# A fused attention, gated layer and mixture of experts: first key load, zero writes, one set of weight bits and the order of attention changed

## Chip, cores and metric

The kernel runs on one core of a Trainium2 chip. The metric is the time of one execution on the device in microseconds, lower is better. Engines are called as in the profile: PE (TensorE), PEld (its weight loads), DVE (VectorE), ACT (ScalarE), POOL (GpSimd), SP (SyncE, which issues most DMAs). A name with a q behind it (SPq, ACTq) is an engine's sequencer, where DMAs are issued.

## What is computed

Three parts run one after the other. Cut to what matters:

```python
# attention: batch 2, heads 8, sequence 576, head size 64, mask by blocks of 64
scores = scale * q @ k^T, hidden where block_i < block_j
attn = exp(scores - max); attn /= sum(attn) + 1e-9
x = (attn @ v) as 1152 tokens x 512
# gated layer, 1536 wide
x = ((x @ w_a) * (x @ w_b)) @ w_out
# mixture: 8 experts, one for each token, capacity 288, 512 -> 1024 -> 512
expert = argmax(x @ w_gate); gate = its softmax weight
rows of x are placed by expert; h = max(x @ w1[e], 0); y = h @ w2[e]
out[token] = gate * y          # zero for tokens beyond the capacity
```

The weights of the gated layer arrive as 64-bit floats and are turned to 32 bits on the chip, by integer operations on the two halves.

## The kernel before

**Attention** treats 8 pairs of heads (pair n, batch n // 4). The steps are written out in the string `ORDER`, one word for each, in the order in which each engine gets its instructions: a word is a letter and indices. `L` loads one tensor of a pair (`load_pair`, L190: queries, keys or values, each with three buffers), `z` scales the queries on ScalarE (L199, not for pair 0), `s` computes scores of one of five row units into one of two PSUM slots, `m` takes the negated maximum on VectorE, `e` the exponential on ScalarE, `r` the reciprocal of the sums, `n` the division on GpSimd, `t` transposes on PE, `h` and `l` copy a transposed tile out of PSUM on ScalarE or VectorE, `p` multiplies with the values, `O` and `P` write the result split into a high and a low part (`xTh`, `xTl`). An engine does its steps in this order and waits where an input or a buffer is not ready. `L01`, the keys of pair 0, is the one load that ScalarE issues, with the constants behind it; all other loads stand in SP's queue.

Steps for the gated layer stand within `ORDER`: `a` loads a pair of column tiles of `w_a` and `w_b` (1 MB, three buffers `raw`), `b` and `c` turn its bits (one ScalarE instruction and four of VectorE, buffers `bits`, two of them), `H` and `I` split the result into high and low parts on ScalarE and GpSimd, and `E`, `A`, `B` compute the first half of the tokens for column tiles 0 to 2 ahead, in the same two PSUM slots as the scores, into `gE`. Before, `a`, `b` and `c` stand there for tiles 0 to 2.

At every third score step of the pairs from 1 on, `clear` (L138) writes zeros from the tile `zrow` in SBUF to a part of `xdisp` (the rows by expert, 2304 x 516) or of the output: nine writes.

**Gated layer, feed-forward** (loop over 12 column tiles f): for f below 3 only the second half of the tokens, two chunks, then four chunks of 288 tokens. A chunk is 24 matmuls of 128x288 (three products of high and low parts, four blocks, two weights), then a copy by ScalarE and a product by VectorE (`gate_mul`). Within the loop the bits of coming tiles are made (`wab_bits`), the splits (`wab_split`), and by the table `plan` at (f, place) the bits of `w_out` (`wout_bits`) and of its transpose (`wot_bits`), from which PE makes the folded gate weights (`gate_rows`, `gate_cols`). Each of the bit steps ends with `load_next`, which issues the next load of the list `later`; three are issued ahead. `raw` and `bits` buffers are shared with these loads.

Then the tokens are projected and their experts chosen, rows are scattered into `xdisp`, and the experts run.

Of the kernel before, what the change touches and what calls it, by code (L numbers as in the profile page):

```python
# [11 lines left out]
F32 = mybir.dt.float32  # L12
# [10 lines left out]
P = 128  # L23

W_MIN = struct.unpack("f", struct.pack("i", 896 << 20))[0]
W_MAX = struct.unpack("f", struct.pack("i", (1150 << 20) + 0xFFE00))[0]
G = 32
NC_IDENT, NC_TRI, NC_IOTA, NC_SEL, NC_TOK = 0, 128, 256, 264, 392


# [1 line left out]


ORDER = """
L10 z1 L01 L00 s01 m01 e010 s02 m02 e011 L11 e020 e021 s00 m00 e000 e001 s04 m04 e040 s03 m03 e030 L02 s12 r01
m12 L12 e031 r00 e120 s11 m11 e121 n010 n011 n001 t04 l04 n000 n021 L20 e111 e110 z2 n020 s10 m10 L22 s14 e101
t03 n031 m14 e140 l03 s13 e100 t02 n030 m13 e130 p05 l02 t01 l01 e131 L21 s21 t00 m21 n040 t06 h06 e210 r11 n101
n111 e211 p06 O00 l00 s20 m20 e201 s24 n110 r10 m24 t05 l05 e200 s23 e240 m23 t14 l14 n120 L30 z3 p00 s22 m22
n100 r21 p01 e231 n140 t15 l15 n130 e230 t10 n121 a0 e220 e221 p02 b0 l10 L31 s31 m31 p03 r20 e310 n131 e311 t11
l11 s32 L40 t13 m32 L41 n201 l13 t12 e321 l12 e320 p04 L32 n221 O01 s30 s34 n200 m30 e301 n210 m34 t16 h16 n220  # L40
n240 t23 P01 s33 p10 n211 P00 p15 p11 t26 n230 l23 m33 n231 e300 r31 n310 n300 e340 t22 l22 z4 s40 l26 s44 e330
m40 e331 m44 e400 t21 r30 n321 e401 t25 s42 p12 e440 p16 n340 l25 p13 O10 a1 m42 e420 l21 n301 s43 e421 P10 m43
p14 O11 P11 t20 h20 t24 l24 L50 e431 s41 e430 n311 t34 l34 z5 m41 e410 n320 L51 e411 r40 p20 n331 t31 t32 p21
l31 s52 n330 n440 b1 t30 l32 t33 m52 e520 e521 r41 n410 l33 s51 m51 p22 n411 p25 n431 h30 c10 p23 p26 p24 O20
P20 n430 s50 m50 n401 O21 L42 t36 h36 e510 t35 L60 e511 l35 e500 s54 m54 e540 P21 t44 l44 t40 e501 z6 s53 p30
m53 e530 n420 e531 l40 p35 p31 L61 s61 n400 r51 m61 e611 L52 t46 t45 h45 e610 l46 n421 p32 L70 r50 c11 n531 s60
m60 t43 e600 l43 n540 e601 n510 s64 m64 e640 t42 h42 t41 h41 p33 p36 p34 O31 s62 c12 s63 m62 n530 t51 P31 t55
O30 p40 l51 e621 e620 t56 h56 p41 n521 P30 p45 p42 z7 n501 n500 n520 m63 e630 c13 L71 s73 m73 n511 h55 p43 p46
e631 r60 n620 n630 O40 p44 O41 t50 l50 t52 h52 s74 r61 n601 e730 t54 t53 P41 p50 n621 n631 l54 e731 H1 I1 t60
m74 e740 l53 s70 m70 e700 n610 e701 P40 s72 m72 e721 L62 e720 p51 p55 p52 n640 l60 s71 m71 e710 e711 c00 p53 p56  # L50
r70 n730 n740 n611 p54 O51 r71 O50 n701 t61 h61 a2 n600 E1100 t62 h62 E1101 c01 E1000 c02 E1102 E1001 b2 E1103
n700 t65 E1110 E1002 E1111 n721 E1003 A10 h65 n731 E1112 E1010 t63 h63 c03 A11 E1113 c20 E1011 H0 P51 t64 P50
h64 E1012 t75 h75 B11 E1013 p60 c21 c22 B10 p65 p61 t70 p62 L72 p66 n720 p63 t66 l66 h70 t71 h71 I0 E0000 E0100
t76 p64 E0101 E0001 t72 c23 E0002 E0102 E0003 E0103 l72 h76 O61 E0010 E0110 O60 P60 E0011 E0111 E0012 E0112 n710
H2 A00 E0013 B00 n711 t74 P61 t73 l73 I2 E2100 E0113 E2101 A01 B01 p70 h74 p75 p71 p76 O70 p72 E2000 p73 E2102
E2001 E2103 E2002 p74 E2003 E2110 E2010 O71 E2111 E2011 P70 E2112 P71 E2012 A21 E2113 B21 E2013 A20 B20
"""

HIDDEN = -1e30
# [2 lines left out]
def const_columns(n_tok, n_exp):  # L62
# [9 lines left out]
    for i in range(P):  # L72
        c[i, NC_SEL + i % G] = 1.0
    c[:, NC_TOK::3] = np.arange(P)[:, None] + P * np.arange(nt)[None, :]
# [1 line left out]


@with_exitstack
def fused_kernel(ctx: ExitStack, tc, shape, q, k, v, w_a, w_b, w_out, w_gate, w1, w2, w_outT, consts, out, cap):
    nc = tc.nc  # L80
    B, H, S, D = shape
    NTOK, DM = out.shape
# [8 lines left out]
    NF = DFF // P  # L91
# [3 lines left out]
    NTT = (S + P - 1) // P  # L95
    ROW = DM + 4
    NSLOT = E * cap
    FAR = 1 << 20
    CH = S // 2
    NCH = NTOK // CH  # L100
    EARLY = 3
# [9 lines left out]

    wgp = cpool.tile([P, KD, G], F32, name="wgp")
    nc.vector.memset(wgp, 0.0)
    xdisp = dpool.tile([NSLOT, ROW], F32, name="xdisp")
# [11 lines left out]
    att1 = es_a.enter_context(tc.tile_pool(name="att1", bufs=1))  # L126
# [2 lines left out]
    psX = es_p.enter_context(tc.tile_pool(name="psX", bufs=2, space=PSUM))  # L129
    psD = es_p.enter_context(tc.tile_pool(name="psD", bufs=1, space=PSUM))  # L130
    psS = es_p.enter_context(tc.tile_pool(name="psS", bufs=1, space=PSUM))


    zrow = att1.tile([P, ROW], F32, name="zrow")
    nc.gpsimd.memset(zrow, 0.0)
    nc.gpsimd.memset(zrow[:, DM + 1:DM + 2], float(FAR))

    def clear(dst, w, r0, cnt):  # L138
        nc.sync.dma_start(
            out=dst[r0:r0 + cnt * P, :].rearrange("(c p) d -> p c d", p=P),  # L140
            in_=zrow[:, 0:w].unsqueeze(1).to_broadcast([P, cnt, w]),
        )

# [44 lines left out]
    def load_pair(n, j):  # L190
        kept, src, w = ((qT, q, NU * P + 2 * ODD), (kT, k, S), (vT, v, NTT * 2 * D))[j]
        kept[n] = att.tile([P, w], F32, tag="qkv"[j], name=f"{'qkv'[j]}T{n}", bufs=3)
        if (n, j) == (0, 1):
            nc.scalar.dma_start(out=kept[n], in_=src[n])
            nc.scalar.dma_start(out=cst, in_=consts)
        else:
            nc.sync.dma_start(out=kept[n], in_=src[n])
# [110 lines left out]
    def pv(n, r):  # L308
# [5 lines left out]
        vt = vT[n].rearrange("p (t c) -> p t c", t=NTT)  # L314
        for m in range(2 * D // G):
            nc.tensor.matmul(
                pxs[n, bank][m * G:(m + 1) * G, a - c0:c1 - c0], lhsT=vt[:, t, m * G:(m + 1) * G],
                rhs=PT[n][:, t, m * G // D, a:c1],
                start=(t == 0), stop=(t == (1, NTT - 1)[bank]), skip_group_check=True,
# [97 lines left out]
        a=load_wab, b=lambda f: bits_wab(f, 0), c=lambda f, i: bits_wab(f, i + 1), H=hi_wab, I=lo_wab,  # L417
        E=ahead, A=ahead_copy, B=ahead_mul,
    )
    clears = [(xdisp, ROW, r, min(3, (NSLOT - r) // P)) for r in range(0, NSLOT - P + 1, 3 * P)]  # L420
    clears += [(out, DM, r, min(3, (NTOK - r) // P)) for r in range(0, NTOK, 3 * P)]
    if NSLOT % P:
        clears.append((xdisp, ROW, NSLOT - P, 1))
    n_score = 0
    for word in ORDER.split():
        steps[word[0]](*map(int, word[1:]))
        if word[0] == "s" and int(word[1]) >= 1:
            if n_score % 3 == 0 and clears:
                clear(*clears.pop(0))
            n_score += 1  # L430
    assert not clears
    nc.sync.dma_start(out=wgp[:, :, 0:E], in_=w_gate.rearrange("(k p) e -> p k e", p=P))
    es_a.close()

# [5 lines left out]

    Wp = gp.tile([P, NF, G], F32, name="Wp")

# [63 lines left out]
    def gate_mul(f, c, pa, pb):  # L506
# [3 lines left out]

    es_p.close()

    later = [
        (load_wab, 3), (load_wab, 4), (load_wab, 5), (load_wot, 0), (load_wab, 6), (load_wout, 0), (load_wab, 7),
        (load_wot, 1), (load_wab, 8), (load_wout, 1), (load_wab, 9), (load_wot, 2), (load_wab, 10), (load_wout, 2),
        (load_wab, 11), (load_wot, 3), (load_wout, 3), (load_wot, 4), (load_wout, 4), (load_wot, 5), (load_wout, 5),
    ]
# [1 line left out]
    def load_next():  # L519
        if later:  # L520
            fn, i = later.pop(0)
            fn(i)

    for _ in range(3):
        load_next()
    nc.sync.dma_start(out=g_sb[:, 0:EARLY, 0:S], in_=gE)

    def wab_bits(f):
        for part in range(5):
            bits_wab(f, part)  # L530
        load_next()

    def wab_split(f):
        hi_wab(f)
        lo_wab(f)

    def wot_bits(c):
        bits_wot(c)
        load_next()

    def wout_bits(c):
# [2 lines left out]


    plan = {
        (2, 3): [(wot_bits, 0)], (3, 1): [(gate_rows, 0), (wout_bits, 0)], (3, 2): [(split_wout, 0)],
        (3, 3): [(gate_cols, 0)],
        (4, 1): [(wot_bits, 1)], (5, 0): [(gate_rows, 1)], (5, 1): [(wout_bits, 1)],
        (5, 2): [(gate_cols, 1), (split_wout, 1)],  # L550
# [8 lines left out]
    with tc.tile_pool(name="psF", bufs=3, space=PSUM) as psF, tc.tile_pool(name="psW", bufs=1, space=PSUM) as psW:  # L559
        for f in range(NF):  # L560
            order = list(range(NCH)) if f >= EARLY else [3, 2]
            for i, c in enumerate(order):
                pp = []
                for j in range(2):
                    ps = psF.tile([P, CH], F32, tag=f"p{j}", name=f"p{j}_{f}_{c}")
                    prod(ps, f, j, c, range(KD))
                    pp.append(ps)
                gate_mul(f, c, *pp)
                place = NCH - len(order) + i
                if i == 0 and f + 3 < NF:  # L570
                    wab_bits(f + 3)
                if i == len(order) - 1 and f + 3 < NF:
                    wab_split(f + 3)
                for fn, x in plan.pop((f, place), ()):
                    fn(x)
            del wab[f]
    assert not plan and not later
    es_x.close()


# [34 lines left out]
    def small(name, shape, dt=F32):  # L615
# [6 lines left out]
        out=tail4[:, :, 1:ROW - DM], in_=cst[:, NC_TOK:NC_TOK + 3 * NT].rearrange("p (t c) -> p t c", c=3)  # L622
# [33 lines left out]
    def place():  # L656
        pp = psG.tile([P, NT + 1, E], F32, tag="pp", name="pp")
        nc.tensor.matmul(pp, lhsT=tri, rhs=oh, start=True, stop=False)
        for t in range(NT):
# [19 lines left out]
        nc.vector.tensor_scalar(  # L679
            out=far, in0=pos, scalar1=float(cap), scalar2=float(FAR), op0=ALU.is_ge, op1=ALU.mult  # L680
        )
# [479 lines left out]
```

## Time and profile before

| | us |
|---|---|
| median of 3 runs | 488.49 |
| lowest, highest | 487.98, 491.27 |
| the profiled execution | 488.28 |
| its span, first to last instruction | 486.5 |
| PE busy | 440.7 |
| DVE busy | 253.5 |
| ACT busy | 191.2 |
| POOL busy | 133.5 |

The profile is of one execution. Times are counted from the first instruction. Busy times of PE hold modelled ends of matmuls, so they are read against the length of a stretch and not as a rate. The granted clock of PE is a share of 2.4 GHz. The chain of work that ended last, which the profile follows back from the last instruction, ends after less than 1 us here, so the stages are read from waits and from windows instead.

### The profile page before, as it was taken

What the parts mean: (1) busy time and instruction counts of PE and PEld (TensorE: products, weight loads), DVE (VectorE), ACT (ScalarE), POOL (GpSimd) and SP (SyncE); (2) the same over time, 40 slices, a digit from 0 to 9 for tenths busy, and PEclk for the clock granted to TensorE, in tenths of its full rate; (3) what the DMA queues carried; (4) which work ended last, traced back from release to release, by engine and by line L of the source; (5) the groups of instructions that cost most, each with busy time, mean ns of one, the idle gap of its engine ahead of it and who ended that gap; (6) DMA issues with size and microseconds to landing.
All of it is one profiled execution on the core that took longest, in us unless ns stands there. A gap on an engine that the chain in (4) does not pass through costs nothing. (4 is left out here: it accounts for less than half of the span.)

```text
span 486.5 us, 8343 instructions
## 1 busy us (share of the span) xinstructions
PE 440.7 (91%) x3248; PEld 358.0 (74%) x3248; DVE 253.5 (52%) x401; ACT 191.2 (39%) x382; POOL 133.5 (27%) x146
## 2 busy tenths in 40 slices
PE   0689999989999699999999999999994999999993
PEld 0245455577799599999999968888883988979750
DVE  0567877784257866676866716221203672826110
ACT  1466667753233344434334322131303563715100
POOL 0067676595011131312221012331212001001000
PEclk9989999999999799999999999999996899999997
DMA  8660971622043545555342000497004983563880
GB/s 275 206 222 8 352 291 33 199 88 86 1 141 110 174 170 174 173 174 172 111 151 88 1 1 0 122 389 292 24 5 128 368 291 126 169 203 111 315 329 11
DMA packets 42986, 76.43 MB, mean 157 GB/s; under 512 B 2850, under 2 KB 15266, under 8 KB 42928
## 3 DMA queue, kind: packets, MB, share of 16 engines
q1 hardware_dynamic: 41296, 71.90, 44.1%
q0 software_dynamic: 1344, 3.29, 1.8%
q8 instruction: 30, 0.49, 0.4%
q10 hardware_dynamic: 288, 0.51, 0.3%
q14 instruction: 28, 0.23, 0.1%
HBM read 64.41 MB, written 11.46 MB: 156 GB/s over the span
## 5 line engine op out<-in xcount | busy, mean ns | idle before, releaser
L395 PE MATMUL p<-xTh,hi 128*128 128x288 f32 x336 | 101.2, 301 | 1.0 <-DVE gE L411 1.0
L395 PE MATMUL p<-xTh,lo 128*128 128x288 f32 x336 | 99.9, 297 | 0.0
L395 PE MATMUL p<-xTl,hi 128*128 128x288 f32 x336 | 99.8, 297 | 0.0
L275 POOL TENSOR_TENSOR PB<-PB,rs 128x128 f32<-128x128 f32 (+4 forms) x72 | 58.4, 842 | 48.1 <-DVE rs L269 47.1
L395 PEld LDWEIGHTS p<-xTh,hi 128*128 128x128 f32 x336 | 64.0, 190 | 4.1 <-issue 2.9
L395 PEld LDWEIGHTS p<-xTl,hi 128*128 128x128 f32 x336 | 64.0, 190 | 0.0
L395 PEld LDWEIGHTS p<-xTh,lo 128*128 128x128 f32 x336 | 63.9, 190 | 0.0
L259 ACT ACTIVATE PB<-sc,nm 128x256 f32<-128x256 f32 (+4 forms) x72 | 39.1, 549 | 34.8 <-DVE nm L249 13.9
L249 DVE TENSOR_REDUCE nm<-sc 128x2 f32<-128x512 f32 (+4 forms) x40 | 32.3, 809 | 32.0 <-PE sc L234 17.3
L388 POOL TENSOR_TENSOR lo<-bits,hi 128x1024 fp32r<-128x1024 f32 x12 | 29.3, 2439 | 65.4 <-ACT hi L382 60.3
L722 PE MATMUL py<-woh,gh 128*128 128x512 f32 x108 | 42.6, 395 | 0.0
L722 PE MATMUL py<-wol,gh 128*128 128x512 f32 x108 | 42.3, 392 | 0.0
L722 PE MATMUL py<-woh,gl 128*128 128x512 f32 x108 | 42.3, 392 | 0.0
L850 PE MATMUL ph<-xt,hi 128*128 128x288 f32 x192 | 41.0, 308 | 0.4 <-ACT xt L817 0.4
L234 PE MATMUL sc<-kT,qT 64*64 64x448 f32 (+7 forms) x256 | 26.9, 471 | 14.7 <-DMA kT<-in_k 11.6
L451 DVE TENSOR_TENSOR gl<-g_sb,gh 128x1536 fp32r<-128x1536 f32 x9 | 15.8, 1756 | 38.4 <-ACT gh L450 38.4
L509 DVE TENSOR_TENSOR g_sb<-asb,p 128x288 f32<-128x288 f32 x42 | 18.8, 451 | 32.2 <-PE p L395 25.8
L835 DVE TENSOR_TENSOR lo<-rawA,hi 128x1024 fp32r<-128x1024 f32 x20 | 24.0, 1224 | 21.7 <-ACT hi L834 21.7
L850 PEld LDWEIGHTS ph<-xt,hi 128*128 128x128 f32 x192 | 33.2, 201 | 1.2 <-ACT xt L817 0.5
L508 ACT COPY asb<-p 128x288 f32<-128x288 f32 x42 | 16.8, 399 | 42.0 <-PE p L395 42.0
L361 POOL TENSOR_TENSOR wol<-wob,woh 128x1024 fp32r<-128x1024 f32 x6 | 14.4, 2399 | 64.3 <-ACT woh L360 53.8
L283 PEld LDWEIGHTS pT<-cst,PB 128*128 128x128 f32 x200 | 22.6, 142 | 12.3 <-issue 5.6
(163 smaller groups left out, 824.3 us busy)
## 6 DMA issues: line engine op xcount, KB each, us to landing
rawA<-in_moe_w SPq DMA_DIRECT2D x18, 1024.0 KB, 8.2
raw<-in_moe_w_a SPq DMA_DIRECT2D x12, 512.0 KB, 4.0
raw<-in_moe_w_b SPq DMA_DIRECT2D x12, 512.0 KB, 5.0
wtr<-in_w_outT SPq DMA_DIRECT2D x6, 1024.0 KB, 5.2
wor<-in_moe_w_out SPq DMA_DIRECT2D x6, 1024.0 KB, 5.0
xdisp<-zrow SPq DMA_DIRECT2D x6, 774.0 KB, 6.0
rawB<-in_moe_w SPq DMA_DIRECT2D x4, 1024.0 KB, 6.6
fs<-in_moe_w SPq DMA_DIRECT2D x4, 1024.0 KB, 10.8
```

What stands on the lines that cost most here:

```text
L234: nc.tensor.matmul(ps[i * BLK:(i + 1) * BLK, h, 512 - w:512 - w + seen], lhsT=qT[n][hs, u * P + i * BLK:u * P + (i + 1) * BLK], rhs=kT[n][ ...
L249: nc.vector.tensor_reduce(out=nm, in_=view, op=ALU.max, axis=ax, negate=True)
L259: nc.scalar.activation(out=dst, in_=src, func=AF.Exp, bias=nms[n][:, c:c + 1], accum_out=SM[n % 2][:, c, 0:1], scale=scale if unscaled(n) ...
L275: nc.gpsimd.tensor_tensor(out=x, in0=x, in1=rss[n, int(bt)][:, c:c + 1].to_broadcast(list(x.shape)), op=ALU.mult)
L283: nc.tensor.transpose(pt[:, j * P:(j + 1) * P], PB[n % 2][:, a:a + P], ident)
L388: nc.gpsimd.tensor_tensor(out=lo, in0=f32(m), in1=f32(hi), op=ALU.subtract)
L395: nc.tensor.matmul(ps, lhsT=wx[:, kd], rhs=xx[:, kd, cs], start=(kd == 0 and n_ == 0), stop=(kd == KD - 1 and n_ == 2),)
L508: nc.scalar.copy(asb, pa)
L509: nc.vector.tensor_tensor(out=g_sb[:, f, c * CH:(c + 1) * CH], in0=asb, in1=pb, op=ALU.mult)
L722: nc.tensor.matmul(s["py"], lhsT=lt[:, f], rhs=rt[:, f], start=(f == 0 and i == 0), stop=(f == NF - 1 and i == 2))
L835: nc.vector.tensor_tensor(out=lo[:, a:a + 2], in0=raw[:, a:a + 2], in1=f32(hi[:, a:a + 2]), op=ALU.subtract)
L850: nc.tensor.matmul(ph[:, 0:cap], lhsT=lt, rhs=rt, start=(n_ == 0), stop=(n_ == len(seq) - 1))
```

## The change

1. `load_pair(0, 0)` and `load_pair(0, 1)`, queries and keys of pair 0, are issued ahead of the first word of `ORDER`, in which they were the fourth and third word.
2. `zrow`, its two fills on GpSimd and the nine writes from it within attention go. The host passes an array `empty` (128 x 516) with the same content; the nine writes are issued from it, DRAM to DRAM, in the feed-forward: one behind each load of `load_next`, from the point where fewer than 14 loads are left.
3. The load and the bits of the fourth column tile (`a3`, `b3`, `c30` to `c33`) are made within attention. In the feed-forward the tiles of `wab_bits` come one step earlier: f + 4 at f = 0 and 1, none at f = 2, and `wot_bits` 0 moves from place (2, 3) to (2, 2).
4. `ORDER` is another permutation of the steps; four copies of transposed tiles go from VectorE to ScalarE.

```diff
-L10 z1 L01 L00 s01 m01 e010 s02 m02 e011 L11 e020 e021 s00 m00 e000 e001 s04 m04 e040 s03 m03 e030 L02 s12 r01
...
+L10 z1 s01 m01 e011 e010 s03 m03 e030 e031 s02 m02 e020 e021 s00 m00 L21 s04 m04 e000 e001 r01 n010 n001 n011
+L11 s13 m13 e040 r00 L20 z2 e130 e131 s10 n040 n020 m10 e101 n021 e100 n000 s14 m14 e140 t04 l04 n031 t06 l06
+s11 m11 e110 t05 l05 s12 e111 m12 t03 h03 r11 e121 t02 s20 m20 a0 L31 e201 s24 l02 m24 L02 e120 r10 n030 e200
+n111 t01 t00 l00 e240 n110 p05 L30 n131 s21 m21 h01 s23 m23 n100 e211 e210 a1 r21 n140 t11 h11 n120 z3 p00 e231
...
+e301 n201 b2 c20 c21 e731 c22 c23 e730 r70 H2 n721 E1100 E1001 E1101 E1002 E1102 l62 I2 E1003 E1103 E1010 A10
...
+h66 E0102 b3 n630 E2002 n730 n701 E0103 n740 A01 E2003 E0110 O51 t61 O50 l61 t65 l65 E2010 c30 n731 E0111 t60 h60
+E2011 E0112 t64 E2012 t76 E0113 P51 p60 n711 P50 l64 p65 c31 l76 p61 p66 p62 E2013 p63 p64 B01 A20 B20 L72 t74
...
-    zrow = att1.tile([P, ROW], F32, name="zrow")
-    nc.gpsimd.memset(zrow, 0.0)
-    nc.gpsimd.memset(zrow[:, DM + 1:DM + 2], float(FAR))
...
+    load_pair(0, 0)
+    load_pair(0, 1)
     for word in ORDER.split():
         steps[word[0]](*map(int, word[1:]))
-        if word[0] == "s" and int(word[1]) >= 1:
-            if n_score % 3 == 0 and clears:
-                clear(*clears.pop(0))
-            n_score += 1
...
+    def clear():
+        dst, w, r0, cnt = clears.pop(0)
+        nc.sync.dma_start(
+            out=dst[r0:r0 + cnt * P, :].rearrange("(c p) d -> p c d", p=P),
+            in_=empty[:, 0:w].unsqueeze(1).to_broadcast([P, cnt, w]),
+        )
...
     later = [
-        (load_wab, 3), (load_wab, 4), (load_wab, 5), (load_wot, 0), (load_wab, 6), (load_wout, 0), (load_wab, 7),
+        (load_wab, 4), (load_wab, 5), (load_wot, 0), (load_wab, 6), (load_wout, 0), (load_wab, 7),
...
             fn(i)
+        if len(later) < 14 and clears:
+            clear()
...
-        (2, 3): [(wot_bits, 0)], (3, 1): [(gate_rows, 0), (wout_bits, 0)], (3, 2): [(split_wout, 0)],
+        (2, 2): [(wot_bits, 0)], (3, 1): [(gate_rows, 0), (wout_bits, 0)], (3, 2): [(split_wout, 0)],
...
-                if i == 0 and f + 3 < NF:
-                    wab_bits(f + 3)
+                ahead_ = 4 if f < EARLY else 3
+                if i == 0 and f != EARLY - 1 and f + ahead_ < NF:
+                    wab_bits(f + ahead_)
                 if i == len(order) - 1 and f + 3 < NF:
                     wab_split(f + 3)
```

## Rows read from the trace of the kernel before

**Rows 1.** Windows by stage: stretch, length, busy us (instructions) by engine, clock, DMA

```profile
12.00:36.00 24.00, 18.07 (x125) 8.08 (x117) 13.94 (x30) 12.85 (x45) 7.83 (x12) 0.93 0.67 220
36.00:98.00 62.00, 58.01 (x654) 31.92 (x655) 48.16 (x90) 42.38 (x127) 41.42 (x51) 1.00 0.52 173
98.00:134.00 36.00, 32.98 (x302) 27.07 (x302) 18.36 (x27) 13.49 (x29) 16.60 (x14) 1.00 0.19 59
172.00:250.00 78.00, 78.00 (x600) 76.28 (x599) 54.35 (x69) 31.65 (x50) 21.48 (x9) 1.00 0.48 155
```

**Rows 2.** Timeline of the start, three engines: start, us, instruction, idle before and releaser

```profile
0.74 0.88 SPq L197 DMA_DIRECT2D qT<-in_q  x2
0.75 1.28 ACT L200 ACT_TABLE_LOAD   x1 [0.75 <-PEq L1122]
3.82 0.74 ACT L200 ACTIVATE qT<-qT 128x640 f32<-128x640 f32 x1 [1.79 <-DMA qT<-in_q]
3.83 0.39 ACTq L194 DMA_DIRECT2D kT<-in_k  x1
11.65 2.41 PE L234 MATMUL sc<-kT,qT 64*64 64x192 f32 x16 [11.65 <-DMA kT<-in_k]
19.57 3.66 PE L234 MATMUL sc<-kT,qT 64*64 64x448 f32 x16
```

**Rows 3.** DMA issues: what, queue, count, KB each, median us from issue to landing

```profile
kT<-in_k ACTq DMA_DIRECT2D x1, 288.0 KB, 7.7
xdisp<-zrow SPq DMA_DIRECT2D x6, 774.0 KB, 6.0
out<-zrow SPq DMA_DIRECT2D x3, 768.0 KB, 9.5
wtr<-in_w_outT SPq DMA_DIRECT2D x6, 1024.0 KB, 5.2
```

**Rows 4.** The tile of queries: the landing of its loads

```profile
DMA to landing us min/median/max: 3.0/3.8/10.1
```

**Rows 5.** Timeline of PE: the wait of the first `gate_rows`

```profile
164.42 1.08 PE L494 MATMUL pw<-wtb,wgp 128*32 128x256 f32 x8 [4.66 <-DVE wtb L355]
```

**Rows 6.** Windows behind that wait

```profile
164.40:166.40 2.00, 1.98 (x12) 1.17 (x13) 1.93 (x4) 0.83 (x2) 0.00 (x0) 0.50 0.34 94
166.40:168.40 2.00, 2.00 (x10) 2.00 (x10) 1.97 (x2) 0.60 (x1) 0.00 (x0) 0.50 1.09 379
168.40:170.40 2.00, 2.00 (x12) 2.00 (x11) 1.93 (x5) 0.40 (x1) 0.00 (x0) 0.58 0.44 82
```

**Rows 7.** Window of attention in which zeros and weights were moved

```profile
48.00:60.00 12.00, 10.82 (x119) 5.86 (x118) 9.24 (x19) 7.60 (x26) 7.45 (x11) 1.00 1.02 333
```

**Rows 8.** Timelines of SP, ACT, DVE, PE: gate part 1 from load to use

```profile
168.66 0.37 SPq L477 DMA_DIRECT2D wtr<-in_w_outT  x1
179.68 1.17 ACT L343 ACTIVATE wtb<-wtr 128x1024 f32<-128x1024 f32 x1
182.80 0.69 DVE L345 TENSOR_SCALAR wtb<-wtb 128x1024 f32<-128x1024 f32 x1
184.25 1.23 DVE L351 SCALAR_TENSOR_TENSOR wtb<-wtr,wtb 128x1024 int32<-128x1024 int32 x1
185.51 1.22 DVE L355 SCALAR_TENSOR_TENSOR wtb<-wtr,wtb 128x1024 int32<-128x1024 int32 x1
190.40 0.64 PE L494 MATMUL pw<-wtb,wgp 128*32 128x256 f32 x8
```

**Rows 9.** Timeline of DVE within attention

```profile
108.85 3.29 DVE L351 SCALAR_TENSOR_TENSOR bits<-raw,bits 128x1024 int32<-128x1024 int32 x1
```

**Rows 10.** Timeline of DVE: last instructions of two sets of bits

```profile
155.69 1.22 DVE L355 SCALAR_TENSOR_TENSOR bits<-raw,bits 128x1024 int32<-128x1024 int32 x1
163.14 1.23 DVE L355 SCALAR_TENSOR_TENSOR wtb<-wtr,wtb 128x1024 int32<-128x1024 int32 x1
```

**Rows 11.** Window of the feed-forward, first matmul to first logits

```profile
134.06:282.97 148.91, 143.64 (x1081) 139.51 (x1081) 103.66 (x126) 57.25 (x91) 36.35 (x18) 0.98 0.41 134
```

## What was predicted

> **What bounds the kernel now.** I read the busy time of the engines by stage first [rows 1]. In each row the reader compares PE's busy time with the length of the stretch. From 36 to 98 us PE is busy 58.01 of 62.00, from 98 to 134 us 32.98 of 36.00, from 172 to 250 us all of it. TensorE is the limit there, and no other engine comes near: VectorE, the next, has 48.16, 18.36 and 54.35. What can be won lies where PE stands still, and the rows of the page add up to three places.
>
> The first is the start. The queues and engines in order of time [rows 2] show that the first matmul of the kernel runs at 11.65, released by the load of `kT`. The cause stands above it: the keys of pair 0 are loaded by ScalarE's queue, and ScalarE issues that load at 3.83, after its scaling of pair 1's queries (step `z1`), which started at 3.82 when those queries landed. The load then takes 7.7 us to land, against 3.0 for the quickest load of queries [rows 3, 4], because everything that SP had issued meanwhile (values, keys, a zero write of 774 KB) shares the DMA engines with it.
>
> The second is the softmax chain of the first pair: 12 to 36 us has 18.07 of 24 busy, with two score slots in PSUM that PE fills and ScalarE empties [rows 1].
>
> The third lies in the feed-forward, which begins at 134.06. At 164.42 the first `gate_rows` has waited 4.66 us for VectorE to end the bits of `wtb` [rows 5]: PE went dry at 159.76. Behind it the granted clock reads 0.50, 0.50 and 0.58 in three windows of 2 us [rows 6], after which it is 1.00 again (2.4 GHz; 0.50 is the 1.2 GHz level).
>
> **First keys ahead of all.** Removed: ScalarE's wait for `z1` before the key load. SP now starts with pair 0's queries, ScalarE with its keys, both at 0.74 to 0.75 as the first DMA and the first ScalarE instruction do in [rows 2]. 288 KB of keys and 320 KB of queries travel together, with pair 1's queries and the constants behind. Bounds for the landing: 3.0 us (the quickest query load) and 7.7 us (this load as it was) [rows 3, 4]. The neighbours are the first query loads, so I take 3.9, which puts the first matmul at 4.65. If the table load (1.28 us) stands ahead of the issue, it is 5.9. I carry 5.0: the start moves by 11.65 - 5.0 = 6.6 us. Bounds: 0.75 + 3.0 = 3.75 (7.9 won) and 0.75 + 1.28 + 7.7 = 9.7 (1.9 won). What is late next: pair 1's first score, which stands in a run of scores at 19.57, 7.9 us after the first one [rows 2], needs `q1` and `k1`. The queue ahead of it (q0, k0, constants, q1, k2, k1, q2) is 2.1 MB, at 333 GB/s [rows 7] 6.4 us: landed by about 9, against some 13. Hidden. Pair 0's values now stand on SP behind the keys of pair 3, whose buffer is free only after pair 0's last score; that score is PE's fifth step of the new order, the first reader of the values its twentieth. I cost it at nothing; if the cover fails, it is one landing, 3.0 us or more.
>
> **Zeros taken out of attention.** The two fills of `zrow` on GpSimd go, and nobody waits for them. Nine writes leave SP's queue there. What loads gain by that can only come out of PE's idle time, which is 4.0 us from 36 to 98 [rows 1]; I take none of it here.
>
> **Fourth weights' bits within attention.** Added there: one ScalarE absolute value, 1.17 us, and four VectorE instructions, 182.80 to 186.73 = 3.9 us undisturbed [rows 8]; the third of the four, 1.23 us there, took 3.29 in attention [rows 8, 9], so 3.9 to 6. They stand at the end of the new order, in 98 to 134 us, where VectorE has 36.00 - 18.36 = 17.6 us free and ScalarE 22.5 [rows 1]. Price zero. Behind them on VectorE's queue the copies of transposed tiles and the products that free PE's score slots; if all the cover were gone, PE would wait up to the longest, 3.3 us.
>
> What it gives back in the feed-forward is a slot. Up to the wait, VectorE makes one set of bits for each of the three half columns: the third set (`bits` of weights 5) ends at 156.9 and the fourth (`wtb`) at 164.4 [rows 10]. Without the first of them `wtb` takes the third slot, since the diff moves it from place (2, 3) to (2, 2). It then ends 156.9 - 134.06 = 22.8 us into the stage. PE asks for it after eight chunks of (159.76 - 134.06) / 8 = 3.21 us, at 25.7 us. Margin 2.9 us, so the wait goes: 4.66 us. One new condition: two `bits` buffers, and the third slot needs the one that GpSimd's subtraction of weights 4 releases. That subtraction starts at the end of the column before, so the slot is not moved by more than the margin. With the wait the slow clock goes. It lasted from 164.4 to about 170.1 (2.0 + 2.0 and 84% of 2.0 us), 5.7 us at half rate, worth 2.8 us. Sum for this part 7.5 us; the stage falls from 148.9 [rows 11] to 141.4. Bounds: 0 (a wait of the same size elsewhere) and 7.5.
>
> **Zeros in the feed-forward.** Six writes of 774 KB and three of 768 KB, 7.1 MB, DRAM to DRAM, one behind each load from the seventh `load_next` on. By the plan these stand at (3, 0), (3, 1), (4, 0), (4, 1), (5, 0), (5, 1), (6, 0), (6, 1), (7, 0): 27 to 81 us into the stage. The weight loads queue behind them. The DMA engines are 0.48 busy from 172 to 250 us [rows 1]. No row shows a DRAM to DRAM copy. From below: 333 GB/s at a share of 1.02 while SBUF zeros and weights were moved [rows 7], 326 GB/s full, so 7.1 MB take 21.8 us of all engines, 0.40 of the 54 us. 0.48 + 0.40 = 0.88: it fits. From above: 9.5 us for each write, the landing of `out<-zrow` [rows 3], taken as if nothing ran beside it, 85 us or 3.9 times that. Then the load is 0.48 + 1.57 = 2.05, and the stage falls 54 x 1.05 = 57 us behind. A delay is felt late: `wtr` of gate 1 was issued at 168.66, lands in 5.2 and was first read at 179.68 (5.8 us spare), and its bits ended at 186.73 for a PE that came at 190.40 (3.7 spare) [rows 3, 8]: 9.5 us in all. I take the lower bound, since both sides of such a copy are long rows as in the loads, and cost it at nothing.
>
> A rule of the Trainium skill speaks against this part: DMA: Bandwidth & Descriptors, section Rules for kernel authors, holds that a zero-stride broadcast of a few copies as the outermost dimension confines a DMA to that many engines. The source is such a broadcast of three, though the code writes the 128 rows outermost. No run here shows which it becomes; by the rule the third rival below would hold, by the rows the sum stays.
>
> **New order.** PE's instructions are the same 200 steps, so its work stays. What an order can change is PE's idle time: 5.9 us in 12 to 36, 4.0 in 36 to 98, 3.0 in 98 to 134, 12.9 in all [rows 1], and it can as well add to it. I take 0 and keep 5 us either way.
>
> **Sum.** 488.28 (the profiled execution; its span is 486.5, and the median of the runs is 488.49) - 6.6 - 7.5 = 474.2. Against the median that is 2.9% less.
>
> **Rivals.**
> (1) The attention gives the start back: the new order's chain of score, maximum, exponential and transposes makes PE wait as much again. For it: 12 to 36 us is bound by that chain and not by PE. Against: 36 to 134 us is 93% PE. Time 488.3 - 7.5 = 480.8.
> (2) The zeros take back what the bits gave. With a copy at 2 times the price of the lower bound the load is 0.48 + 0.80 = 1.28, the stage falls 54 x 0.28 = 15 us behind, less 9.5 spare is a wait of 5.6 us, with slow clock behind it again about 7.5. Time about 481.7. Against: one engine's time goes by bytes in every row.
> (3) Slower: the zeros make the feed-forward wait for DMA. It decides from the point where the backlog is 14.1 + 9.5 = 23.6 us, that is from 1 + 23.6/54 = 1.44 of load, a price of 2.4 times. On three engines out of 16 it is 5.3 times: 0.48 + 2.1 on those, 54 x 1.6 = 86 us behind, 77 of wait, some 550 us. For it: no copy of this kind is in the trace, and the nine writes stand in one FIFO with the weights. Against: the same shape from SBUF reached 333 GB/s together with loads.
> (4) More: the order also takes 5 of the 12.9 us of idle. 469.
>
> **Chances.** Forecast 0.60, (1) 0.13, (2) 0.12, (3) 0.06, (4) 0.09. The forecast's own range is 470 to 478: 1 us of the start to the good, 3 of it and of the order to the bad. The range reaches down to (4) and up past (1) and (2): 468.5 to 482.5. About 1% (4.9 us) is what a measurement of this kernel can tell from no change, so faster means under 483.6. Forecast, (4), 0.8 of (1) and 0.6 of (2) lie there: 0.87; within 1% 0.07; slower, rival (3), 0.06.
>
> **What the profile after would show.** Start: the first L234 matmul at about 5 instead of 11.65, still released by `kT`; above 8 the landing was mis-sized. Order: the first feed-forward matmul at about 127.5; at 134 rival (1). Bits: no wait of PE for `wtb`, clock 1.00 behind it, the stage 141 to 142 us long. Zeros: landing of `xdisp<-empty` under 10 us, and loads of `wtr` read without a wait; waits of PE for `wtb` or of ScalarE for a DMA there show (2) or (3). Everything behind the feed-forward should keep its length; if it does not, the sum is wrong in a place that I did not look at.

## The result, and the profile after

The changed kernel takes 471.88 us (median; 470.74 to 472.54), the one before 488.56 beside it. The ratio is 0.9651 with a 95% interval of 0.9613 to 0.9689, so 3.5% less. The forecast was 474.2, its range 468.5 to 482.5. The profiled execution of after took 472.4 us, 15.9 less than the one that the sum was made against.

The windows by stage come first. Columns are the stretch, its length, busy us (instructions) of PE, PEld, DVE, ACT and POOL, the granted clock of PE, the DMA engines' mean share and GB/s. They answer to [rows 1] and, in the last line, to [rows 11].

```profile
12.00:36.00 24.00, 19.90 (x141) 9.96 (x145) 12.97 (x28) 13.42 (x44) 12.78 (x18) 0.73 0.38 124
36.00:98.00 62.00, 55.79 (x644) 34.59 (x637) 48.38 (x87) 46.10 (x133) 37.12 (x47) 1.00 0.37 118
98.00:126.00 28.00, 27.23 (x269) 22.98 (x268) 13.55 (x25) 8.06 (x18) 10.35 (x12) 1.00 0.21 69
126.18:267.80 141.62, 141.03 (x1080) 137.38 (x1080) 101.23 (x122) 56.99 (x90) 36.68 (x18) 1.00 0.57 184
```

The last line is the feed-forward. It is 141.62 us long instead of 148.91 and PE is busy in 141.03 of them, at full clock: the one wait of PE that is left is 0.6 us at its end. Its DMA share is 0.57 instead of 0.41, which is the zeros. The third line ends where the feed-forward begins, 7.88 us earlier than before (134.06). In the second, PE stands still 6.2 us instead of 4.0; in the third 0.8, where before it was 3.0.

The timeline of the start (start, us, queue or engine, instruction, in brackets the idle time before and what ended it), which answers to [rows 2]:

```profile
0.75 0.40 ACTq L185 DMA_DIRECT2D kT<-in_k  x1
0.75 0.90 SPq L188 DMA_DIRECT2D qT<-in_q  x2
1.18 0.45 ACTq L186 DMA_DIRECT2D cst<-consts  x1
1.66 1.28 ACT L191 ACT_TABLE_LOAD   x1 [1.66 <-PEq L1124]
5.07 2.83 PE L225 MATMUL sc<-kT,qT 64*64 64x192 f32 x16 [5.07 <-DMA qT<-in_q]
6.27 0.74 ACT L191 ACTIVATE qT<-qT 128x640 f32<-128x640 f32 x1 [3.33 <-DMA qT<-in_q]
12.03 2.29 PE L214 MATMUL sc<-kT,qT 128*128 128x288 f32 x4 [0.60 <-DVE nm L240]
```

The keys go out at 0.75, ahead of ScalarE's table load, and the first matmul runs at 5.07 instead of 11.65. In this execution the queries landed last and released it; in other kernels with the same first loads (e4, e6, e7, e9) the keys did.

The timeline of the bits of `wtb` in the feed-forward, with the subtraction on GpSimd beside them, and the matmul that reads them (its line of the waits is gone; before, PE stood still 4.66 us there [rows 5]):

```profile
140.21 2.40 POOL L379 TENSOR_TENSOR lo<-bits,hi 128x1024 fp32r<-128x1024 f32 x1 [3.81 <-ACT hi L373]
142.63 1.19 ACT L334 ACTIVATE wtb<-wtr 128x1024 f32<-128x1024 f32 x1 [1.43 <-POOL lo L379]
145.78 1.23 DVE L342 SCALAR_TENSOR_TENSOR wtb<-wtr,wtb 128x1024 int32<-128x1024 int32 x1
146.62 2.65 POOL L379 TENSOR_TENSOR lo<-bits,hi 128x1024 fp32r<-128x1024 f32 x1 [4.02 <-ACT hi L373]
147.04 3.31 DVE L346 SCALAR_TENSOR_TENSOR wtb<-wtr,wtb 128x1024 int32<-128x1024 int32 x1
151.81 0.64 PE L477 MATMUL pw<-wtb,wgp 128*32 128x256 f32 x8
```

The bits end at 147.04 + 3.31 = 150.35, 24.2 us into the stage, and PE comes for them at 151.81, 25.6 us into it. They are in time by 1.5 us.

The DMA issues of the zeros (what, queue, count, KB each, median us from issue to landing), and the stretch of 60 us in which they travel, in the columns of the windows:

```profile
xdisp<-empty SPq DMA_DIRECT2D x6, 774.0 KB, 9.2
out<-empty SPq DMA_DIRECT2D x3, 768.0 KB, 8.1
```

```profile
155.00:215.00 60.00, 60.00 (x462) 58.86 (x461) 43.56 (x55) 24.89 (x39) 16.53 (x7) 1.00 0.88 281
```

The DMA engines are busy 0.88 of that stretch, at 281 GB/s, and PE all of it.

### The profile page after: what moved, and what is told of

The parts are those of the page before. It is cut to its first block, busy times and chain, and to the rows that moved or that the text cites. A ratio compares the mean times of both kernels' runs of the same rounds, so it can differ in the third digit from the quotient of the medians.

```text
span 470.6 us, 8325 instructions
## 1 busy us (share of the span) xinstructions
PE 435.6 (93%) x3248; PEld 357.4 (76%) x3248; DVE 249.1 (53%) x397; ACT 193.3 (41%) x386; POOL 126.8 (27%) x144
## 5 line engine op out<-in xcount | busy, mean ns | idle before, releaser
L386 PE MATMUL p<-xTh,hi 128*128 128x288 f32 x336 | 100.1, 298 | 0.6 <-DVE gE L402 0.6
L266 POOL TENSOR_TENSOR PB<-PB,rs 128x128 f32<-128x128 f32 (+4 forms) x72 | 53.3, 769 | 47.9 <-DVE rs L260 44.8
L386 PEld LDWEIGHTS p<-xTh,hi 128*128 128x128 f32 x336 | 63.0, 188 | 3.3 <-issue 2.5
L225 PE MATMUL sc<-kT,qT 64*64 64x64 f32 (+7 forms) x256 | 25.5, 467 | 12.1 <-ACT PB L250 7.0
L274 PE MATMUL pT<-cst,PB 128*128 128x128 f32 x200 | 30.1, 284 | 0.9 <-ACT PT L297 0.8
```

Of the source, the lines that this page charges most:

```text
L225: nc.tensor.matmul(ps[i * BLK:(i + 1) * BLK, h, 512 - w:512 - w + seen], lhsT=qT[n][hs, u * P + i * BLK:u * P + (i + 1) * BLK], rhs=kT[n][ ...
L266: nc.gpsimd.tensor_tensor(out=x, in0=x, in1=rss[n, int(bt)][:, c:c + 1].to_broadcast(list(x.shape)), op=ALU.mult)
L274: nc.tensor.transpose(pt[:, j * P:(j + 1) * P], PB[n % 2][:, a:a + P], ident)
L386: nc.tensor.matmul(ps, lhsT=wx[:, kd], rhs=xx[:, kd, cs], start=(kd == 0 and n_ == 0), stop=(kd == KD - 1 and n_ == 2),)
```

## Experiments

All are told by three times: the median of the runs, the start of the first feed-forward matmul (T0), and the length of the feed-forward from there to the first logits (`pl`), the last two from the one profiled execution of each. The row of before gives the range of the medians of its four sets of runs. Executions of kernels that are alike up to T0 (after, e5, e8, e9, e10) have it between 125.37 and 126.27, so smaller differences than 0.9 us at T0 say little.

| | median us (range) | ratio to before, 95% | T0 | feed-forward |
|---|---|---|---|---|
| before | 488.05 to 488.95 | 1 | 134.06 | 148.9 |
| after | 471.88 (470.74 to 472.54) | 0.9613 to 0.9689 | 126.18 | 141.6 |
| e7 keys alone | 480.78 (479.50 to 481.90) | 0.9791 to 0.9866 | 128.52 | 147.8 |
| e1 keys as before | 477.50 (476.51 to 478.93) | 0.9718 to 0.9810 | 131.51 | 141.7 |
| e2 bits as before | 479.50 (478.75 to 480.61) | 0.9762 to 0.9851 | 126.16 | 148.8 |
| e3 old order | 474.49 (473.86 to 475.38) | 0.9664 to 0.9754 | 128.01 | 141.7 |
| e4 zeros in attention | 472.01 (471.43 to 472.36) | 0.9613 to 0.9699 | 125.55 | 141.7 |
| e5 zeros twice | 502.11 (501.56 to 503.07) | 1.0239 to 1.0306 | 125.81 | 170.0 |
| e8 zeros twice, apart | 473.96 (471.87 to 476.43) | 0.9647 to 0.9738 | 125.37 | 143.3 |
| e9 copies outermost | 518.47 (518.14 to 519.10) | 1.0564 to 1.0640 | 126.27 | 187.9 |
| e6 warm clock | 471.12 (468.91 to 472.54) | 0.9609 to 0.9676 | 123.04 | 141.7 |
| e10 after again | 472.23 (471.27 to 473.07) | 0.9625 to 0.9681 | 125.96 | 141.7 |
| e11 warm from start | 469.71 (468.84 to 470.25) | 0.9579 to 0.9633 | 122.71 | 141.7 |

### The keys

The kernel before with this part of the change alone (e7), and the kernel after without it (e1).

```diff
 # e7, on the kernel before
-L10 z1 L01 L00 s01 ...
+L10 z1 s01 ...
+    load_pair(0, 0)
+    load_pair(0, 1)
     for word in ORDER.split():
 # e1, on the kernel after
-L10 z1 s01 ...
+L10 z1 L01 L00 s01 ...
-    load_pair(0, 0)
-    load_pair(0, 1)
```

> The kernel before with one part of the change alone: first queries and keys ahead of the order. Sum of the prediction: 488.5 - 6.6 = 481.9. Rival (parts of the gain need the others, such as the zeros gone from the queue or the new order): 484 or more.

> The changed kernel, but the first queries and keys stand in the order again as fourth and third word (L10 z1 L01 L00). Sum of the prediction: the first matmul is back at 11 to 12 us, everything behind moves by 6.6 us, 478.5 us against 471.9 of the changed kernel. Rival (the attention would have given the start back, bound by something later): 474 or less.

The first matmul of e7, by the timeline of PE, and then of e1 the two loads that SP issues just before the keys, the issue of the keys, and the first matmul:

```profile
4.91 2.41 PE L234 MATMUL sc<-kT,qT 64*64 64x192 f32 x16 [4.91 <-DMA kT<-in_k]
```

```profile
3.09 0.43 SPq L359 DMA_DIRECT2D raw<-in_moe_w_a  x1
3.62 0.46 SPq L359 DMA_DIRECT2D raw<-in_moe_w_b  x1
3.63 0.40 ACTq L185 DMA_DIRECT2D kT<-in_k  x1
10.44 2.84 PE L225 MATMUL sc<-kT,qT 64*64 64x192 f32 x16 [10.44 <-DMA kT<-in_k]
```

Alone, the keys bring the first matmul forward by 6.7 us (11.65 to 4.91), T0 by 5.5 us (134.06 to 128.52) and the kernel by 8.1 us of medians (488.91 beside it). So 1.2 us of the start were given back within attention, a small part of rival (1). The feed-forward of e7 is 1.1 us shorter, and its rows show where. These are PE's wait for `wtb` and the two windows behind it:

```profile
158.89 1.08 PE L496 MATMUL pw<-wtb,wgp 128*32 128x256 f32 x8 [4.66 <-DVE wtb L355]
158.87:160.87 2.00, 1.98 (x12) 1.18 (x13) 1.93 (x4) 0.84 (x2) 0.00 (x0) 0.50 0.30 88
160.87:162.87 2.00, 2.00 (x13) 2.00 (x13) 1.97 (x2) 0.74 (x2) 0.00 (x0) 0.71 1.08 377
```

The wait is as long as before, but the lower clock behind it lasts 3.2 us (2.0 and 58% of 2.0) where the prediction read 5.7 in the kernel before [rows 6]; half of the difference is 1.2 us. Why it ended sooner is not shown. The rest of the 8.1 us lies behind the feed-forward (0.8 in the profiled executions) and in the spread of the runs. The expectation was 481.9, and 480.78 was measured.

In the new kernel the late keys cost 5.3 us at T0, all of the 5.4 us by which the first matmul is later; 478.5 was expected and 477.50 measured. There the keys land at 10.44 and not at 11.65, though they are issued at 3.63, about as late as before. What travels beside them differs: no zero write and no values stand in SP's queue, but 1 MB of weights, issued just before. Which of these brings them in sooner was not tested.

### The bits

```diff
 # e2, on the kernel after: a3 b3 c30 c31 c32 c33 out of ORDER, and
+        (load_wab, 3), (load_wab, 4), (load_wab, 5), (load_wot, 0), ...
-        (2, 2): [(wot_bits, 0)], ...
+        (2, 3): [(wot_bits, 0)], ...
+                if i == 0 and f + 3 < NF:
+                    wab_bits(f + 3)
```

> The changed kernel, but the fourth weights' load and bits are made in the feed-forward again, as before (plan and the load list too). Sum of the prediction: PE waits some 4.7 us for wtb again and then runs at the slow clock for some 5.7 us, 7.3 us in all: 479.2. Rival (what the bits cost in attention comes back, so that the part is worth less): 474 to 476.

The wait of PE is back, by the timeline of PE and the window of the feed-forward in e2:

```profile
156.53 1.08 PE L455 MATMUL pw<-wtb,wgp 128*32 128x256 f32 x8 [4.67 <-DVE wtb L324]
126.16:274.93 148.77, 143.48 (x1081) 139.35 (x1081) 103.91 (x126) 57.23 (x91) 36.37 (x18) 0.98 0.55 182
```

The wait is 4.67 us, as it was 4.66 before, and the eight matmuls behind it take 1.08 instead of 0.64 us. The stage is 7.1 us longer than after's, the median 7.5 above that of e4, which was timed beside it; 479.2 was expected and 479.50 measured. T0 does not move (126.16): within attention these bits cost nothing. The zeros are in this stage as well (share 0.55), so the wait and its removal have nothing to do with them.

### The order

```diff
 # e3, on the kernel after: ORDER of before, without L01 L00, and
-... c03 A11 ... E0100 t76 ... E0102 E0003 ... E0110 O60 ... E0112 n710 ... B01 p70 ...
+... c03 a3 A11 ... E0100 b3 t76 ... E0102 c30 E0003 ... E0110 c31 O60 ... E0112 c32 n710 ... B01 c33 p70 ...
```

> The changed kernel with the order of before, the first loads ahead of it and the new steps a3, b3 and c30 to c33 put in near its end. Prediction (the order is worth nothing): 471.9 to 473.2, since the start moved by 6.6 us and the feed-forward's begin by 7.9. Rival (the new order carries a part of what the start gave): 475 to 479.

T0 is 128.01, 1.8 us later than after's; the median is 2.5 above that of e4, which was timed beside it and does not overlap it. The new order is worth about 2 us, and the expected 471.9 to 473.2 was too little. The old order also takes back the engine of 36 copies of transposed tiles: in the new one 20 of them had gone from VectorE to ScalarE and 16 the other way, four more on ScalarE in all. So the order and the place of the copies are tested together. The window of the tail of attention in e3, and then all from the first matmul to T0, in e3 and in after:

```profile
98.00:128.01 30.01, 27.06 (x257) 21.37 (x257) 18.16 (x24) 10.13 (x20) 11.95 (x10) 1.00 0.33 106
5.00:128.01 123.01, 109.53 (x1080) 67.81 (x1080) 86.02 (x150) 70.35 (x201) 66.18 (x75) 0.97 0.35 117
```

```profile
5.07:126.18 121.11, 107.07 (x1080) 69.05 (x1080) 78.76 (x146) 71.87 (x205) 60.24 (x75) 0.94 0.36 118
```

In the tail PE stands still 3.0 us, as in the kernel before, against 0.8 in after. From 36 to 98 it is the other way round (58.03 busy in e3, 55.79 in after). From the first matmul to T0 the idle time is about the same in both, 13.5 and 14.0, and what is won lies in PE's busy time, 109.5 and 107.1, which holds modelled ends. How the order wins them is not settled.

### The zeros

First their place: `zrow` and its nine writes back in attention, none in the feed-forward, everything else as after (e4).

```diff
+    zrow = att1.tile([P, ROW], F32, name="zrow")
...
+        if word[0] == "s" and int(word[1]) >= 1:
+            if n_score % 3 == 0 and clears:
+                clear(*clears.pop(0))
...
-        if len(later) < 14 and clears:
-            clear()
```

> The changed kernel, but the zeros are written from SBUF within attention as before, none in the feed-forward. Prediction (zeros cost nothing in either place once the first keys are ahead of them): 471.9, within 1. Rival A (they delayed loads in attention): 474 or more. Rival B (DRAM to DRAM zeros cost in the feed-forward): 470 or less.

The same stretch of the feed-forward without zeros, in e4:

```profile
155.00:215.00 60.00, 60.00 (x462) 58.86 (x461) 42.94 (x54) 25.23 (x40) 17.14 (x8) 1.00 0.53 175
```

The median is 472.01, as expected, and the stage is 141.7 us long: the place of the zeros changes nothing that can be measured. In the feed-forward they raise the DMA share from 0.53 to 0.88 and the rate from 175 to 281 GB/s, and PE has 60.00 busy of 60.00 in both. Both places hide them.

Then their price, by making each write twice: to the same place (e5), and to other memory (e8).

```diff
 # e5
+        for _ in range(2):
             nc.sync.dma_start(out=dst[r0:r0 + cnt * P, :]...
 # e8
+    scr = [dpool.tile([3 * P, ROW], F32, name=f"scr{i}") for i in range(9)]
...
+        nc.sync.dma_start(
+            out=scr[len(clears)][0:cnt * P, 0:w].rearrange("(c p) d -> p c d", p=P),
+            in_=empty[:, 0:w].unsqueeze(1).to_broadcast([P, cnt, w]),
+        )
```

> The changed kernel, each of the nine zero writes issued twice in the feed-forward. By the prediction's own formula (0.40 of the DMA engines for each set): load 0.48 + 0.80 = 1.28, 15 us behind, less 9.5 us spare is 5.6 us of PE waiting, with the slow clock 477 to 480. Rival (a delay is absorbed further than I counted, since the loads' readers wait without PE noticing): 472 to 473. Rival (such a copy costs more than its bytes): above 485.

> The changed kernel with a second write of zeros of the same size behind each of the nine, into other memory that nobody reads, so that SP does not wait for the first to land as it did with zeros written twice to one place (502.1, SP 7 to 10 us in each pair). By the prediction's formula the DMA engines would be loaded 1.28 for 54 us, 15 us behind, less 9.5 spare: 5.6 us of PE waiting, 477 to 480. Rival (the 30 us were the price of such copies and not of SP's wait): 490 or more. Rival (absorbed): 472 to 473.

e5 missed its expectation by over 20 us. SP's own queue in e5 shows why, by three of its pairs and by the line of its waits (us in total, times, longest):

```profile
155.04 7.34 SPq L506 DMA_DIRECT2D xdisp<-empty  x2
163.63 9.72 SPq L506 DMA_DIRECT2D xdisp<-empty  x2
174.06 10.59 SPq L506 DMA_DIRECT2D xdisp<-empty  x2
SPq L506 <- DMA xdisp<-empty: 49.2, 6, 9.5
```

A pair of writes to the same rows holds SP for 7 to 11 us, where one issue takes 0.57 in after: by the line of the waits SP stands until the first has landed, 49.2 us for the six pairs of `xdisp`, and every weight load behind stands still with it. The waits that follow are ScalarE's for `wtr` and PE's for `wtb` (19.2 us in two). So e5 measured a wait in a queue and not the price of the copies. e8 has no such wait and gives the price, by its window and by the rows at its one wait of PE for `wtb` (ScalarE, GpSimd, VectorE, PE):

```profile
155.00:215.00 60.00, 60.00 (x462) 58.86 (x461) 42.84 (x54) 24.86 (x39) 16.65 (x7) 1.00 1.06 350
222.06 1.12 ACT L335 ACTIVATE wtb<-wtr 128x1024 f32<-128x1024 f32 x1 [4.93 <-DMA wtr<-in_w_outT]
225.74 2.41 POOL L380 TENSOR_TENSOR lo<-bits,hi 128x1024 fp32r<-128x1024 f32 x1 [8.27 <-ACT hi L374]
225.94 3.30 DVE L347 SCALAR_TENSOR_TENSOR wtb<-wtr,wtb 128x1024 int32<-128x1024 int32 x1
229.38 0.64 PE L478 MATMUL pw<-wtb,wgp 128*32 128x256 f32 x8 [1.57 <-DVE wtb L347]
```

Twice the bytes make the stage 1.7 us longer in the profiled execution. The runs alone do not separate e8 from after: 471.87 to 476.43 against 471.27 to 473.07 of e10, timed beside it. The median of 473.96 lies under the 477 to 480 that the formula gave and far under the 490 of the rival. The loads are late, as the formula says: ScalarE waits 4.93 us for `wtr`. But the bits now fall beside a subtraction of GpSimd, and the last VectorE instruction takes 3.30 us where it takes 1.23 alone [rows 8]. These 2.1 us are more than PE's 1.6, so by these rows (an estimate) the late load alone would still have been covered. The formula with the rate that was reached comes out near: 7.1 MB in 60 us are 118 GB/s, so the loads and two sets of copies ask for 175 + 2 x 118 = 411 GB/s, and the engines move 350; they fall 60 x 61 / 350 = 10.5 us behind, 1.0 more than the 9.5 us of spare that the prediction had counted. It is rough, since one set by the same sum makes 293 GB/s and 281 was measured, and it does not hold the VectorE instruction.

Last the dimension of the broadcast: the three copies outermost (e9), on the kernel after.

```diff
-            out=dst[r0:r0 + cnt * P, :].rearrange("(c p) d -> p c d", p=P),
-            in_=empty[:, 0:w].unsqueeze(1).to_broadcast([P, cnt, w]),
+            out=dst[r0:r0 + cnt * P, :].rearrange("(c p) d -> c p d", p=P),
+            in_=empty[:, 0:w].unsqueeze(0).to_broadcast([cnt, P, w]),
```

> The changed kernel, but in each zero write the three copies are the outermost dimension and the 128 rows the second. The Trainium skill (DMA: Bandwidth & Descriptors, Rules for kernel authors) says that this confines a write to three engines: then those three are loaded 2.6 times, PE waits some tens of us, above 500, and the writes land after 12 us or more. Rival (the dimensions are put in another order on the way to the DMA engines): as the changed kernel, 471 to 473.

The window of e9, PE's waits, and SP's queue:

```profile
155.00:215.00 60.00, 47.61 (x359) 46.34 (x358) 32.54 (x42) 17.69 (x28) 13.90 (x6) 0.95 0.47 164
PE pw L477 <- DVE wtb L346: 26.9, 3, 12.6
174.30 11.08 SPq L505 DMA_DIRECT2D xdisp<-empty  x1
193.75 10.90 SPq L359 DMA_DIRECT2D raw<-in_moe_w_b  x1
217.98 17.55 SPq L359 DMA_DIRECT2D raw<-in_moe_w_a  x1
```

The same bytes from the same array to the same rows, and the kernel is 6% slower than before. The mean share of the 16 engines falls to 0.47 while the queue is late, and issues in the queue hold SP for 11 to 17.6 us. The records of single packets in the traces tell how few engines that is. In after the six writes to `xdisp` are 2304 packets of 2064 bytes. In e9 they are 108 packets of 44,032 bytes, 1.63 us each, and of the 60 us in which any of them is under way, three are at once in 57 and never more than three but for 0.3 us. For 42 us those three are all that the DMA engines have under way, where in after 16 or 17 packets at once are most common. The records do not name the engine, but by that count these writes went over three of them. Byte for byte such a packet is no slower than the small ones (27 GB/s against 24 for a packet of 2064 bytes in 0.085 us), so it is not their size that makes them slow. The three writes to `out` cannot be told apart by size, and the trace of e9 has no landing of the writes to set against the 12 us expected. This is rival (3), which did not come because the kernel writes the 128 rows outermost. The Trainium skill, page DMA: Bandwidth & Descriptors, section Rules for kernel authors, asks for a dimension such as the 128 partitions outermost; these two runs agree, 518.5 us against 472.2 beside it. The stage grew by 46 us where the rival had 77 of wait. The rival let the whole delay fall into 54 us, while here the copies went on draining as the stage grew; that this is the whole difference is not shown.

### The clock at the start

The four matmuls of score step `s04` take 2.29 us in after, and those of the same step two pairs later 1.24 us:

```profile
28.48 1.24 PE L214 MATMUL sc<-kT,qT 128*128 128x288 f32 x4 [1.08 <-ACT PB L250]
```

PE runs the first ones at the 1.2 GHz level, in a stretch where it often stands still for the softmax. e6 puts 20 matmuls whose result nobody reads into its gaps, e11 eight more ahead of the first score (the profile counts each as two); e10 is after again, beside e11.

```diff
 # e6; in e11 also warm(8) ahead of the loop over ORDER
+    wt = psD.tile([P, 512], F32, tag="px1", name="warm")
+    wz = wgp.rearrange("p k g -> p (k g)")
+    def warm(k):
+        for _ in range(k):
+            nc.tensor.matmul(wt[:, 0:P], lhsT=wz, rhs=wz, start=True, stop=True)
-... s02 m02 ... s00 m00 ... s13 m13 ... s10 n040 ...
+... s02 W7 m02 ... s00 W2 m00 ... s13 W4 m13 ... s10 W7 n040 ...
```

> The changed kernel with 20 additional matmuls of zeros (128x128, into an unused PSUM bank) put into PE's gaps between the scores of pairs 0 and 1; their result is not used. Theory: the slow clock from 11.5 to 25 us in the changed kernel comes from PE's sparse work in 8 to 12 us and costs 3 to 5 us; with the gaps filled the clock stays at 1.00: 467 to 469. Rival (the softmax chain sets the time there, not PE): 471 to 472. Rival (zeros do not hold the clock): clock 0.50 as before and 472 to 474.

> The changed kernel as it is, timed again beside the next run on the same chip: 471 to 472.5.

> The changed kernel with matmuls of zeros in PE's gaps between the scores of pairs 0 and 1, as in the run that kept the s04 matmuls at 1.24 instead of 2.29 us, and with 8 more ahead of the first score. Theory (PE's slow clock up to 25 us costs some 3 us of the softmax chain): the feed-forward begins at 122 to 123, 468 to 469. Rival (the gain of 3 us that one profiled run showed is lost again behind attention): 471 to 472.

The timeline of PE at `s04` and at T0, first of e10, then of e11:

```profile
11.99 2.29 PE L214 MATMUL sc<-kT,qT 128*128 128x288 f32 x4 [0.59 <-DVE nm L240]
125.96 0.40 PE L386 MATMUL p<-xTh,hi 128*128 128x288 f32 x1 [0.58 <-DVE gE L402]
```

```profile
1.07 3.78 PE L389 MATMUL warm<-wgp 128*128 128x128 f32 x16 [1.07 <-DVE wgp L93]
11.63 1.24 PE L192 MATMUL sc<-kT,qT 128*128 128x288 f32 x4
122.71 0.40 PE L364 MATMUL p<-xTh,hi 128*128 128x288 f32 x1 [0.58 <-DVE gE L380]
```

With the filling from the start, `s04` takes 1.24 us, T0 is 3.3 us earlier and the kernel 2.5 us faster than e10 beside it (468.84 to 470.25 against 471.27 to 473.07). So e11 is faster than both kernels: 0.9606 of before, 0.9579 to 0.9633. The T0 expected for it was 122 to 123 and came; the 469.71 us are a little over the 468 to 469 expected. e6 missed its 467 to 469 by the median (471.12; the runs, 468.91 to 472.54, cover after's range), though its profiled execution has the same 1.24 us and a T0 of 123.04.

## Why the prediction was right, step by step

The parts put in one after another, each kernel having one more (the profiled executions):

| | T0 | feed-forward | whole |
|---|---|---|---|
| before | 134.06 | 148.9 | 488.28 |
| + keys (e7) | 128.52 | 147.8 | 480.85 |
| + bits and zeros (e3) | 128.01 | 141.7 | 474.79 |
| + order (after) | 126.18 | 141.6 | 472.4 |

The forecast took 14.1 us off the profiled execution of before, and 15.9 came off. The start brought 1.1 less to T0 than the 6.6 carried (5.5), the bits 0.2 less than their 7.5, the order 1.8 instead of 0; 0.5 more came off T0 between e7 and e3, and 0.7 behind the feed-forward. The smaller of these are within what executions differ by. That the whole is so near is in part luck: what the start lacked hides more than half of what the order gave.

**Start, 6.6.** Right in size and cause at the first matmul: 5.07 against 5.0 carried, 6.58 won. The landing was taken from the row of the first query loads, which was the right neighbour. Two details were off: in after the release came from the queries and not from the keys, and the table load stands behind the issue. Of 6.7 us at the first matmul of e7 5.5 reached T0, so in the old order rival (1) holds for about a sixth of it; in the new order (e1) 5.3 of 5.4 did. No wait of PE for the values of pair 0 appears.

**Bits, 7.5.** The stage fell by 7.3 us and the wait is gone, by the mechanism named: one set less in front, and `wtb` in the third slot. e2 brings all of it back. The margin was mis-sized: 2.9 us predicted, 1.5 found, mostly because the last VectorE instruction took 3.31 us and not 1.23, which is 2.1 us; the other steps made up some of it. The slower price was in the rows for attention [rows 9] and was not carried over to the feed-forward. The condition named, the buffer that GpSimd's subtraction releases, did come last (142.63, behind 140.21 + 2.40), and did not use up the margin. The part of the clock, 2.8 us, rests on one execution: by their windows the lower clock behind the same wait lasted 5.7 us in before, 5.3 in e2 and 3.2 in e7.

**Zeros, 0.** Right, and by the load that was worked out: 0.48 + 0.40 = 0.88, measured 0.88. That it fits to the hundredth is luck: the terms were taken for other stretches, and in the 60 us shown it is 0.53 without zeros (e4) and 0.35 for them. Landing is 8.1 to 9.2 us, and no load is waited for. e4 shows the nothing directly. Rival (2) was too dear: at twice the price it gave 7.5 us of loss, and e8 shows 1.7. The engines reached 350 GB/s there, where 326 was taken as full, and what PE did wait hung on a VectorE instruction slowed beside GpSimd as well.

**Order, 0.** This term was mis-sized, by about 2 us: e3 gives 1.8 us at T0, within the bound of 5. Its reasoning failed too. The prediction held that an order can change only PE's idle time, 12.9 us of it [rows 1]; between e3 and after the idle time did not fall (13.5 and 14.0 us), and PE's busy time did, by 2.5. Nor was the start's clock in the sum: PE runs the first scores at the lower level, and e11 took 2.5 us off by filling its gaps.

**Behind the feed-forward** the kernel kept its length, but for 0.7 us less.

## What to carry to other kernels

Look for what stands ahead of the first load on the engine that issues it: a step that waits for another load costs the whole kernel its wait, though some of the gain can be lost again where a dependent chain follows (1.2 of 6.7 us in e7, none in e1). A stall late in a stage can be removed by moving an equal piece of work on the same engine into a stage where that engine has time, and is worth the slow clock behind it as well. Before bulk writes are put into a queue of loads, compare the bytes of the stretch with the best rate that any row shows, and look at the outermost dimension and at what the issue itself may wait for: both cost more here (46 and 28 us) than the bytes (1.7 us for twice as many).

## What the runs showed of the hardware

**The granted-clock column cannot be trusted at the start.** By the timeline and the window of e1 the four matmuls of `s04` take 2.29 us while the column reads 1.00; in after, it reads 0.50 for matmuls of the same duration (two lines of e1, one of after):

```profile
17.65 2.29 PE L214 MATMUL sc<-kT,qT 128*128 128x288 f32 x4 [0.59 <-DVE nm L240]
16.50:20.00 3.50, 2.91 (x16) 1.46 (x20) 0.65 (x4) 1.23 (x4) 0.00 (x0) 1.00 0.00 0
```

```profile
12.03:14.24 2.21, 2.21 (x4) 1.17 (x4) 0.14 (x1) 0.02 (x1) 0.00 (x0) 0.50 0.00 0
```

The duration of a fixed group of matmuls tells the level better than the column: 2.29 us at the lower, 1.24 at the upper. The Trainium skill, page TensorE: Matmul & The Clock Gate, section Seeing it yourself, warns that the clock events of a trace have been observed to be unreliable; e1 and e4 agree (1.00 beside 2.29 us in both). In the kernel before they took 2.29 us too, at 17.35, so the 0.93 of the first line of [rows 1] hid a slow clock that the prediction did not see.

**VectorE beside GpSimd.** The same instruction on the same shape takes 1.23 us alone [rows 8] and 3.31 while GpSimd subtracts two tiles in SBUF. In after it happens to the set of bits before `wtb` as well, beside the subtraction from 140.21 to 142.61, and in e8 at 225.94:

```profile
140.31 3.38 DVE L346 SCALAR_TENSOR_TENSOR bits<-raw,bits 128x1024 int32<-128x1024 int32 x1
```

Each time the instruction ends 1.1 us after GpSimd's does, about the 1.2 us that it takes alone. The one before it, at 145.78, had started ahead of GpSimd's and took 1.23 us. The Trainium skill, page SBUF — State Buffer, section Who interferes with whom, says that a VectorE instruction with two inputs in SBUF contends with a GpSimd instruction that reads SBUF; the trace of after agrees, with 146.62 + 2.65 = 149.27 as the end of the one and 150.35 of the other.

**Copies from DRAM to DRAM go by their bytes.** 7.1 MB of them, 118 GB/s over the 60 us, raised the rate from 175 to 281 GB/s and the share from 0.53 to 0.88; twice as many gave 350 GB/s at 1.06. In all three a full share is 319 to 330 GB/s. Where a second write went to the same rows (e5), SP stood until the first had landed, for 7 to 11 us a pair; to other memory (e8) it did not. Whether the program or the queue asks for that wait was not tested.
